# One-core channel attention with two gated layers: output products in teams from the fourth double block of layer one on, and periods in new orders

## The chip, the core and the metric

The kernel runs on one core of one Trainium2 chip, as one launch. The metric is the device time in microseconds. Five engines take part: TensorE (PE, with its weight loads PEld), VectorE (DVE), ScalarE (ACT), GpSimd (POOL) and SyncE (SP, which only issues DMAs). Each works through its own list in order, and semaphores tie the lists together.

## What is computed

```python
qn = q / (norm(q, axis=1) + 1e-6);  kn = k / (norm(k, axis=1) + 1e-6)
a = softmax(kn.transpose(0, 2, 1) @ qn / tau)        # 256 x 256, over 6016 tokens
x = v @ a                                            # 6016 x 256
xn = x / sqrt(mean(x * x) + 1e-6) * rms_g
y = (silu(xn @ w_gate) * (xn @ w_val)) @ w_out       # layer one, 256 -> 1536 -> 256
out = (sigmoid(y @ w_gate2) * (y @ w_val2)) @ w_out2 # layer two, the same sizes
```

All of it is fp32. A product is made of three matmuls (function `mm3`): each operand is split into a high part, rounded to fp32r, and a low part, the rest, and high by high, high by low and low by high are summed in one PSUM bank.

## The kernel before

**Tiling.** The tokens are cut into six double blocks of 2 x 512 columns (the third, of index 2, has 2 x 448), the hidden width of 1536 into twelve slices f of 128. One **period** handles one slice of one double block.

**Gate and value products by seven for eight.** For a double block, gate and value of a slice need eight products; `period` makes them with seven. PE runs them in the order 11, S1, (the fourth product of the period before), T2, 12, T3, S4; bank Z takes 11, T2, T3 one upon the other, bank B takes S1 and S4. Between them Z is read out: ACT copies it into A (L747, after 11), into g1 (L772, after T2) and into D (L792, after T3); then DVE adds Z and e5, the copy of B, into v1 (L798), and B into g1 (L804). ACT turns g1 into a gate (L733), and DVE multiplies gates and values (L551, L553). The next period's 11 goes into the bank Z that v1 has read, its S1 into the bank that the addition into g1 has read: PSUM has two banks `g` for Z and B, two `v`, two `y` and two `at`.

**Output products.** Double blocks 0 and 1 of layer one run plainly, block by block. Double blocks 2 to 5 of layer one run in periods whose output products are plain: four a period (`out_mm`), of two split values (L750, L775), 33 matmuls a period with the seven. In layer two the output products are made in **teams**: a team is six slices (half a double block), and its 3 x 7 products stand for 3 x 8. They follow in the six periods of the next half, 3 in an odd period and 4 in an even one, 31.5 matmuls a period on average. Each needs a source of its own: ACT casts it to its high part (L618, `split_high`), DVE subtracts to get the low part (L626, `split_low`). Sums of sources are made by DVE (`first_sum`, L559) or by DMAs that accumulate, issued by POOL (`more`, L571). `gather` adds the products into the result tiles r, and `send` (L652) stores them. The double blocks of layer two run in the order 0, 1, 3, 4, 5, 2.

**What surrounds it.** The weights of layer two come from DRAM for every slice (`gw_load`, L500, two DMAs of 448 KB, into three buffer pairs), those of the teams' output products by `ow_load` (L584). The operands of the next double block are loaded in its predecessor's first period (`pair_load`), three sums of them are made on POOL after the third (`pair_sums`, L398), a fourth later, and they are split one by one (`pair_high` L366, `pair_low` L369). During layer one, six loads `out_load` bring in the output weights of layer two, ACT and DVE split them, POOL sums them, and they are stored in `od`. The order of all this is the order of the statements in `period`; `slots` hang further work on named points of it.

Of the kernel before, what the change touches and what calls it, by code (L numbers as in the profile page):

```python
# [25 lines left out]
def kernel(  # L26
# [71 lines left out]
    gd = [dram.tile([P, 2, NG, P], F32, name=f"gd{f}") for f in range(NF)]  # L98
    rd = [dram.tile([P, 4, P], F32, name=f"rd{i}") for i in range(NF // 2)]
    od = [dram.tile([P, 8, 2, NJ, P], F32, name=f"od{g}") for g in range(2)]  # L100
# [24 lines left out]
    def conversion(l, f):  # L125
# [45 lines left out]
        def sums():  # L171
            t = w["t"]
            if l:
                nc.sync.dma_start(out=rd[f // 2][:, f % 2 * 2 : f % 2 * 2 + 2], in_=t[:, OUT:])
# [42 lines left out]
        def stored():  # L217
            if l:
                nc.sync.dma_start(out=gd[f][:, 0], in_=f32(w["h"]))
                nc.sync.dma_start(out=gd[f][:, 1], in_=f32(w["l"]))  # L220
# [217 lines left out]
    def hidden(name):  # L438
        return ip3.tile([P, 512], F32R, tag=name, name=name)
# [49 lines left out]
    stream0 = [(0, p, f) for p in range(PLAIN, NP) for f in range(NF)]  # L489
    stream1 = [(1, p, f) for p in (0, 1, 3, 4, 5, 2) for f in range(NF)]  # L490
    stream = stream0 + stream1
    HALF = NF // 2
    teams = [(p, g) for _, p, f in stream1[::NF] for g in range(2)]
    gw = {}

    def gw_load(n):
        if n < len(stream1):
            gw[stream1[n]] = [wp.tile([P, NG, P], F32R, tag=f"w{e}{n % 3}", name="gw") for e in "hl"]
            for e, t in enumerate(gw[stream1[n]]):
                nc.sync.dma_start(out=f32(t), in_=gd[stream1[n][2]][:, e])  # L500

    def product(ps, it, i, a, start, stop=True):
# [4 lines left out]
        ch, cl = gw[it] if l else (wh[0, f], wl[0, f])  # L507
# [4 lines left out]
    def out_load(i):  # L512
        odd["t"] = sp.tile([P, 4, P], F32, tag="t1", name="ot")
        nc.sync.dma_start(out=odd["t"], in_=rd[i])

    def out_store(i, h, lo, first):
        g, j = divmod(i, NJ)
        for e, t in enumerate((h, lo)):
            nc.sync.dma_start(out=od[g][:, first : first + 4, e, j], in_=f32(t))

    def out_split(i):
        odd["h"] = sp.tile([P, 4, P], F32R, tag="t2", name="oh")
        nc.scalar.copy(odd["h"], odd["t"])

    def out_low(i):
        lo = sp.tile([P, 4, P], F32R, tag="ol", name="ol")
        nc.vector.tensor_sub(lo, odd["t"], f32(odd["h"]))
        out_store(i, odd["h"], lo, 0)

    def out_sums(i):  # L530
        w11, w21, w12, w22 = (odd["t"][:, u] for u in range(4))
# [4 lines left out]

    def sums_low(i):
        lo = sp.tile([P, 4, P], F32R, tag="ol", name="ol")
        nc.vector.tensor_sub(lo, odd["t"], f32(odd["h"]))
        out_store(i, odd["h"], lo, 4)  # L540
# [14 lines left out]
    def first_sum(n):  # L555

        w = hw[stream1[n][1]]
# [3 lines left out]
    def third_sum(n):  # L561

        w = hw[stream1[n][1]]
# [15 lines left out]
    def ow_load():  # L579
        i, k = divmod(ow_n[0], len(KINDS))  # L580
        if i < len(teams):
            tag = ("wh3", "wl3", "wh4", "wl4")[ow_n[0] % 4]
            t = wp.tile([P, 2, NJ, P], F32R, tag=tag, name="ow")
            nc.sync.dma_start(out=f32(t), in_=od[teams[i][1]][:, PLACE.index(KINDS[k])])  # L584
# [7 lines left out]
    def team_start(i):  # L592

        p, g = teams[i]
        w = hw[p]
        if g == 0:
# [8 lines left out]
            p=p, g=g, w=w, split=0, done=0, parts={},  # L605
# [5 lines left out]
    def split_high(ahead):  # L611
        while job and job["split"] < min(LAST, job["done"] + ahead):
            i = job["split"]
            k, j = divmod(i, NJ)
            a, b, c, d = job["h"][j]
            src = xs[job["x"] + j][:, : job["w"]] if KINDS[k] == "S1" else {"12": c, "S4": d, "S3": b}.get(KINDS[k], a)
            h, lo = (hidden(t)[:, : job["w"]] for t in ("hh", "hl"))
            nc.scalar.copy(h, src)  # L618
            job["parts"][i] = h, lo
            job["split"] += 1  # L620
            lows.append((i, h, lo, src))

    def split_low():
        while lows:
# [25 lines left out]
    def send(v, c, e, t):  # L650
        p, w = v["p"], v["w"]
        nc.sync.dma_start(out=out_t[c * P : (c + 1) * P, p0[p] + e * w : p0[p] + (e + 1) * w], in_=t)  # L652
# [37 lines left out]
    def period(it, pv, n, outs=()):  # L690


        s = {}
        slot = slots.popleft() if slots else {}
        outs = deque(partial(out_mm, *o, c) for o in outs for c in range(KC))
        n1 = n - len(stream0)
# [5 lines left out]
        def fourth(s):  # L702
            l, p, f = s["it"]
            w = hw[p]
            product(s["v0"], s["it"], T4, A22, False)
            gated(s["h"][:, 0, :w] if l else s["v0"], s["v0"], s["sg0"], l and f % 2)

        def split(ahead):
            if n1 >= 0:
                split_high(ahead)  # L710
                split_low()

        def out(count):
            for _ in range(count):
                if outs:
                    outs.popleft()()
                elif n1 >= 0:
                    out_product()

        if it:  # L720
            l, p, f = it
            w = hw[p]
            s["it"] = it
            act = (AF.Silu, AF.Sigmoid)[l]
            Z = gv_bank("g")[:, :w]
            product(Z, it, B11, A11, True)
            A = gv_bank("v")[:, :w]
            B = gv_bank("g")[:, :w]
            product(B, it, T1, S1, True)
        if pv:  # L730
            pl, pp, pf = pv["it"]
            pw = hw[pp]
            nc.scalar.activation(out=pv["g1"], in_=pv["g1"], func=(AF.Silu, AF.Sigmoid)[pl])  # L733
            gated(pv["v1"], pv["v1"], pv["g1"], pl and pf % 2 == 0)
        flush()
        if n1 > 0 and n1 % HALF == 0:
            team_start(n1 // HALF - 1)
        if n1 > 0 and pf % 2:
            third_sum(n1 - 1)
        split(2)  # L740
        if not it:
            while job["done"] < LAST:
                split(3)
                out_product()
                flush()
            return
        nc.scalar.copy(A, Z)  # L747
        if pv and pl == 0:
            hh1, hl1 = hidden("hh"), hidden("hl")
            nc.scalar.copy(hh1[:, :pw], pv["v1"])  # L750
            nc.vector.tensor_sub(hl1[:, :pw], pv["v1"], f32(hh1[:, :pw]))  # L751
            hid[pl, pp, 1, pf] = hh1, hl1
            fourth(pv)
        e5 = sp.tile([P, 512], F32, tag="e5", name="e5")[:, :w]
        if pv and pl:
            nc.scalar.copy(e5, B)
            if n1 > 0:
                split_high(3)
            fourth(pv)
            gw_load(n1 + 2)  # L760
            split_low()
            if pf % 2 == 0:
                first_sum(n1 - 1)
        at("early")
        if not (pv and pl):
            nc.scalar.copy(e5, B)
        else:
            out(1 if n1 % 2 == 0 else 0)
# [4 lines left out]
        if pv and pl == 0:  # L773
            hh0, hl0 = hidden("hh"), hidden("hl")
            nc.scalar.copy(hh0[:, :pw], pv["v0"])  # L775
            nc.vector.tensor_sub(hl0[:, :pw], pv["v0"], f32(hh0[:, :pw]))
            hid[pl, pp, 0, pf] = hh0, hl0
        flush()
        if n1 % 2 == 0:
            split(3)  # L780
        if n1 >= 0:
            out(2 if outs else 1)
            at("DVE")
        s["sg0"] = ip2.tile([P, 512], F32, tag="sg", name="sg")[:, :w]
        nc.scalar.activation(out=s["sg0"], in_=A, func=act)  # L785
        if n1 < 0:
            out(2)
            at("ACT")
            at("DVE")
# [3 lines left out]
        if l:  # L793
            s["h"] = h_tile()
            s["v1"] = s["h"][:, 1, :w]
        else:
            s["v1"] = sp.tile([P, 512], F32, tag="t0", name="v1")[:, :w]
        nc.vector.tensor_add(s["v1"], Z, e5)  # L798
        flush()
        if n1 >= 0:  # L800
            split_high(3)
            at("ACT")
        product(B, it, B22, S4, False)
        nc.vector.tensor_add(s["g1"], s["g1"], B)  # L804
        split_low()
        if n == len(stream) - 1:
            out(2)
            fourth(s)
        else:
            out(max(2, len(outs)))  # L810
        at("end")
        return s

    with tc.manual_schedule():
# [255 lines left out]

        pv = None
        outs = [(0, b // 2, b % 2, f) for b, f in items[-SKEW:]]
        for n, it in enumerate([*stream, None]):
            if it and it[2] == 0:
                slots.clear()
                slots.extend({} for _ in range(NF))
                if n <= len(stream0):
# [12 lines left out]
            if 6 <= n < 6 + 6 * NF // 2 and n % NF % 6 == 0:  # L1090
                i = n // 6 - 1
                slots[0].setdefault("end", []).append(partial(out_load, i))
                slots[1].setdefault("ACT", []).append(partial(out_split, i))
# [55 lines left out]
```

## Time and profile before

| | us |
|---|---|
| median of three runs (lowest, highest) | 1226.77 (1225.41, 1227.59) |
| the profiled execution's own time | 1227.86 |
| its span, first to last instruction | 1225.8 |
| PE busy in the span | 1178.7 (96%) |
| DVE, ACT, POOL busy | 911.7, 847.5, 281.1 |

The span is cut below at ACT's copy L772 of the first period of each double block, so that one stretch holds twelve periods. "x397" is a count of instructions that touch the stretch, one more than belong to it.

### The profile page before, as it was taken

How to read it: one execution, taken by the hardware profiler on the slowest of the kernel's cores; microseconds unless marked ns; L12 is line 12 of the kernel's file. 1: busy time of each engine (PE TensorE's matmuls, PEld its weight loads, DVE VectorE, ACT ScalarE, POOL GpSimd, SP SyncE). 2: the span in 40 equal slices, each digit the busy share in tenths (PEclk: the TensorE clock that was granted, in tenths of full speed). 3: DMA queues.
4: the chain of work that ended last, by engine and by line, in shares of the span. 5: the costliest groups of instructions: out<-in, count | busy, mean ns of one | idle time of the engine just before them, and what ended most of it. 6: DMA issues, size and time to landing. Idle time of an engine off the chain costs nothing.

```text
span 1225.8 us, 15986 instructions
## 1 busy us (share of the span) xinstructions
PE 1178.7 (96%) x5290; PEld 966.1 (79%) x5290; DVE 911.7 (74%) x1382; ACT 847.5 (69%) x1591; POOL 281.1 (23%) x327
## 2 busy tenths in 40 slices
PE   8898999999999999999999999999999999999997
PEld 7787777788899788888888677777777777778895
DVE  6798888876566566666665577887887888887877
ACT  6665667765566676677666677677777777777775
POOL 0043655553200200200200111311311311311121
PEclk9899999999999999999999999999999999999999
DMA  9662434766301301201430578988988988988995
GB/s 334 245 221 87 131 107 158 260 224 207 111 1 28 97 26 35 95 26 35 155 99 1 168 200 248 263 247 244 267 251 239 275 246 239 277 239 248 271 251 140
DMA packets 100946, 214.43 MB, mean 175 GB/s; under 512 B 10240, under 2 KB 35840, under 8 KB 100864
## 3 DMA queue, kind: packets, MB, share of 16 engines
q1 hardware_dynamic: 86896, 188.65, 46.2%
q0 software_dynamic: 13824, 24.65, 11.1%
q8 instruction: 41, 0.67, 0.2%
q14 instruction: 41, 0.34, 0.1%
q10 hardware_dynamic: 144, 0.13, 0.0%
HBM read 150.87 MB, written 37.88 MB: 154 GB/s over the span
## 4 chain that ended last, share of the span: by engine, by line
PE 62%; DVE 11%; ACT 4%; issue 4%; DMA 1%; POOL 0%; SPq 0%; DVEq 0%; ACTq 0%; POOLq 0%
PE g L107 10%; PE g L108 9%; PE g L109 9%; PE v L107 4%; PE v L108 4%; PE y L108 4%; PE v L109 4%; PE y L109 4%; PE y L107 4%; PE at L108 3%; PE at L109 3%; PE at L107 3%; DVE hl L626 2%; DVE g L804 2%; ACT v L792 1%
## 5 line engine op out<-in xcount | busy, mean ns | idle before, releaser
L571 POOL DMA_DIRECT2D hs<-hs x96 | 83.6, 914 | 466.1 <-DVE hl L626 197.3
L626 DVE TENSOR_TENSOR hl<-hs,hh 128x512 fp32r<-128x512 f32 (+1 forms) x216 | 152.5, 714 | 20.5 <-ACT hh L618 19.7
L733 ACT ACTIVATE g<-g 128x512 f32<-128x512 f32 (+1 forms) x120 | 74.7, 623 | 121.9 <-DVE g L804 121.9
L618 ACT CAST hh<-hs 128x512 fp32r<-128x512 f32 (+1 forms) x216 | 130.1, 609 | 4.6 <-PE y L109 1.4
L792 ACT COPY v<-g 128x512 f32<-128x512 f32 (+1 forms) x120 | 67.2, 560 | 65.8 <-PE g L109 65.1
L772 ACT COPY g<-g 128x512 f32<-128x512 f32 (+1 forms) x120 | 69.4, 578 | 44.7 <-PE g L109 44.0
L798 DVE TENSOR_TENSOR hs<-g,e 128x512 f32<-128x512 f32 (+1 forms) x72 | 48.9, 680 | 50.1 <-ACT v L792 50.1
L804 DVE TENSOR_TENSOR g<-g,g 128x512 f32<-128x512 f32 (+1 forms) x120 | 79.7, 664 | 0.0
L107 PE MATMUL g<-xh,gw 128*128 128x512 f32 x180 | 73.0, 405 | 5.7 <-DVE hs L798 4.9
L785 ACT ACTIVATE sg<-v 128x512 f32<-128x512 f32 (+1 forms) x120 | 71.1, 592 | 3.7
L107 PE MATMUL g<-qh,wh 128*128 128x512 f32 x168 | 66.8, 397 | 6.6 <-ACT wh L187 5.3
L798 DVE TENSOR_TENSOR v<-g,e 128x512 f32<-128x512 f32 (+1 forms) x48 | 32.4, 675 | 53.9 <-ACT v L792 53.9
L747 ACT COPY v<-g 128x512 f32<-128x512 f32 (+1 forms) x120 | 68.0, 567 | 4.8 <-PE g L109 0.3
L108 PE MATMUL g<-xl,gw 128*128 128x512 f32 x180 | 70.3, 391 | 0.0
L109 PE MATMUL g<-xh,gw 128*128 128x512 f32 x180 | 70.2, 390 | 0.0
L109 PE MATMUL g<-qh,wl 128*128 128x512 f32 x168 | 66.3, 395 | 1.9 <-DVE wl L196 1.9
L108 PE MATMUL g<-ql,wh 128*128 128x512 f32 x168 | 66.0, 393 | 0.0
L108 PE MATMUL y<-hl,ow 128*128 128x512 f32 (+1 forms) x144 | 57.2, 397 | 9.1 <-DVE hl L626 9.0
L451 ACT CAST hh<-v 128x512 fp32r<-128x512 f32 x48 | 28.1, 585 | 48.5 <-DVE v L449 48.5
L107 PE MATMUL v<-qh,wh 128*128 128x512 f32 x144 | 57.9, 402 | 3.3 <-DVE hl L457 3.3
L751 DVE TENSOR_TENSOR hl<-v,hh 128x512 fp32r<-128x512 f32 (+1 forms) x48 | 32.7, 681 | 32.4 <-ACT hh L750 32.4
L109 PE MATMUL v<-qh,wl 128*128 128x512 f32 x144 | 56.6, 393 | 0.0
(230 smaller groups left out, 3650.2 us busy)
## 6 DMA issues: line engine op xcount, KB each, us to landing
gw<-gd SPq DMA_DIRECT2D x144, 448.0 KB, 5.5
ow<-od SPq DMA_DIRECT2D x84, 384.0 KB, 5.1
hs<-hs POOLq DMA_DIRECT2D x80, 256.0 KB, 6.7
wraw<-in_w_dram SPq DMA_DIRECT2D x24, 768.0 KB, 5.4
vraw<-in_v_t_dram SPq DMA_DIRECT2D x11, 512.0 KB, 3.8
gd<-w2h SPq DMA_DIRECT2D x12, 448.0 KB, 2.6
gd<-w2l SPq DMA_DIRECT2D x12, 448.0 KB, 3.5
yd<-yo SPq DMA_DIRECT2D x20, 256.0 KB, 2.9
```

What stands on the lines that cost most here:

```text
L107: nc.tensor.matmul(ps, sh, mh, start=start, stop=False, skip_group_check=more)
L108: nc.tensor.matmul(ps, sh, ml, start=False, stop=False, skip_group_check=more)
L109: nc.tensor.matmul(ps, sl, mh, start=False, stop=stop, skip_group_check=more)
L571: nc.gpsimd.dma_start(out=to, in_=t, accum_op=ALU.add)
L618: nc.scalar.copy(h, src)
L626: nc.vector.tensor_sub(lo, src, f32(h))
L733: nc.scalar.activation(out=pv["g1"], in_=pv["g1"], func=(AF.Silu, AF.Sigmoid)[pl])
L772: nc.scalar.copy(s["g1"], Z)
L785: nc.scalar.activation(out=s["sg0"], in_=A, func=act)
L792: nc.scalar.copy(D, Z)
L798: nc.vector.tensor_add(s["v1"], Z, e5)
L804: nc.vector.tensor_add(s["g1"], s["g1"], B)
```

## The change

The teams now begin at double block 3 of layer one: three double blocks more. Of the ten that run in periods, double block 2 of layer one alone keeps `period` and the plain output products; the other nine go through `team_period`, which reads the order of its steps from a table: EVEN and ODD by the period's number, NONE in the first six periods, where there is no team yet. So:

- The three double blocks need 54 matmuls fewer: PE's list has 5137 in place of 5191. For each of their six teams they need the casts, low parts, sums and gathers that teams need. In all, ACT gets 72 instructions more, DVE 114, POOL 72 (48 of them accumulating DMAs), SP 180 DMAs.
- Layer one's weights for the slices are stored to DRAM during double block 2 (`store_w`) and loaded per slice like layer two's; its output weights are summed and split there too, six loads more.
- Sources are split up to four products ahead, with four buffers each for high and low parts, where it was two or three products and three buffers. A call of `split_high` or `split_low` handles one source, and the table has seven or so calls a period.
- In the first six periods every odd one uses the banks `at` for Z and B.
- The loads of layer two's output weights are moved: one at the end of slice 9 and one at the end of slice 11, split one period later.

```diff
-    stream0 = [(0, p, f) for p in range(PLAIN, NP) for f in range(NF)]
-    stream1 = [(1, p, f) for p in (0, 1, 3, 4, 5, 2) for f in range(NF)]
+    alone = [(0, PLAIN, f) for f in range(NF)]
+    joint = [(0, p, f) for p in range(PLAIN + 1, NP) for f in range(NF)]
+    joint += [(1, p, f) for p in (0, 1, 3, 4, 5, 2) for f in range(NF)]
...
-        return ip3.tile([P, 512], F32R, tag=name, name=name)
+        return ip3.tile([P, 512], F32R, tag=name, name=name, bufs=4)
...
-    def split_high(ahead):
-        while job and job["split"] < min(LAST, job["done"] + ahead):
-            i = job["split"]
+    def split_high():
+        if not job or job["split"] >= min(LAST, job["done"] + 4):
+            return
+        i = job["split"]
...
+    EVEN = (
+        "part1 gate 11 h1 gw S1 cpA lo hi third hi P4 flush lo"
+        " e5 early first T2 12 h0 cpG hi lo sg lo flush hi out"
+        " DVE lo T3 part0 cpD ACT hi S4 v1 end g1 hi lo out"
+        " out hi lo out"
+    ).split()
...
+        def bank(j):
+            return (at_bank, j) if n < HALF and n % 2 else (gv_bank, "g")
...
+        for step in (EVEN, ODD)[n % 2] if n >= HALF else NONE:
+            do.get(step, partial(at, step))()
...
+            if 0 < n // NF < 4 and f == NF - 3:
+                u = 2 * (n // NF - 1)
+                slots[0].setdefault("end", []).append(partial(out_load, 1, u))
+                out_weights(1, u, slots[1], slots[2])
+                slots[2]["end"].append(partial(out_load, 1, u + 1))
+            if 1 < n // NF < 5 and f == 0:
+                out_weights(1, 2 * (n // NF - 1) - 1, slots[0], slots[1])
```

In the table's words, hi and lo are one call of `split_high` and `split_low`, P4 is the fourth product of the period before, cpA, cpG, cpD are ACT's three copies of Z, h0 and h1 the two gated values of the period before, out is one output product, end, early, ACT and DVE are the points for the slots.

**First place: ACT in two periods without output products.** Before, in layer two's first double block (v is A or D, e5 the copy of B, g1 and sg the two gates):

```order
L747 COPY v_6618<-g_6614 128x512
L756 COPY e5_6626<-g_6619 128x512
L772 COPY g1_6644<-g_6614 128x512
L785 ACTIVATE sg_6646<-v_6618 128x512
L792 COPY v_6651<-g_6614 128x512
L366 CAST qh_6499<-xs_6608 128x512
L733 ACTIVATE g1_6644<-g1_6644 128x512
L747 COPY v_6664<-g_6660 128x512
```

Now, in double block 3 of layer one:

```order
L807 COPY v_4374<-at_4366 128x512
L841 ACTIVATE g1_4345<-g1_4345 128x512
L807 COPY e5_4384<-at_4370 128x512
L807 COPY g1_4396<-at_4366 128x512
L365 CAST xh_4248<-xs_4357 128x512
L816 ACTIVATE sg_4399<-v_4374 128x512
L807 COPY v_4404<-at_4366 128x512
L807 COPY v_4420<-g_4412 128x512
```

Z and B of this period lie in `at`, those of the next in `g` again, and the gate stands behind the copy into A instead of ahead of it.

**Second place: POOL about the three sums of the next double block's operands** (the accumulating DMAs are of `hs`, the sums `xs`), in double block 1 of layer two. Before:

```order
L571 DMA hs_6824<-hs_6896 128x512
L571 DMA hs_6977<-hs_7048 128x512
L571 DMA hs_7126<-hs_7196 128x512
L398 TENSOR_TENSOR xs_7460<-xl_7304,xl_7294 128x512
L398 TENSOR_TENSOR xs_7462<-xl_7306,xs_7460 128x512
```

Now:

```order
L566 DMA hs_7478<-hs_7557 128x512
L566 DMA hs_7927<-hs_8023 128x512
L566 DMA hs_7629<-hs_7710 128x512
L397 TENSOR_TENSOR xs_8094<-xl_7940,xl_7930 128x512
L397 TENSOR_TENSOR xs_8096<-xl_7942,xs_8094 128x512
L397 TENSOR_TENSOR xs_8098<-xl_7942,xl_7940 128x512
L566 DMA hs_7778<-hs_7849 128x512
```

Before, the sums stood behind the accumulation of the last of the three sources of kind S2 (hs_7126); now they stand behind that of the second (hs_7629) and ahead of that of the third.

**Third place: DVE beside these sums.** Now, from the low part that the accumulation into hs_7629 waits for (hl are low parts, hs_8023<-v_8018 is h0, hs_8092<-g_8040 is v1, g1_8074 the addition into g1, the last row is h1):

```order
L622 TENSOR_TENSOR hl_8056<-hs_7629,hh_8055 128x512
L546 SCALAR_TENSOR_TENSOR hs_8023<-v_8018,sg_8009 128x512
L812 TENSOR_TENSOR hs_8092<-g_8040,e5_8065 128x512
L845 TENSOR_TENSOR g1_8074<-g1_8074,g_8049 128x512
L622 TENSOR_TENSOR hl_8087<-hs_7778,hh_8086 128x512
L622 TENSOR_TENSOR hl_8112<-hs_7557,hh_8111 128x512
L546 SCALAR_TENSOR_TENSOR hs_8092<-hs_8092,g1_8074 128x512
```

Three instructions that read PSUM follow the low part, and only then two further low parts. What stood there before is shown with its times in the rows below (rows 5): a low part, h0, a low part, a sum of two sources, v1.

## Rows read from the trace of the kernel before

**Rows 1.** The page: busy time, share of the span and instructions of each engine.

```profile
PE 1178.7 (96%) x5290; PEld 966.1 (79%) x5290; DVE 911.7 (74%) x1382; ACT 847.5 (69%) x1591; POOL 281.1 (23%) x327
```

**Rows 2.** Stretches: length, busy us (instructions) by engine, granted clock, DMA share, GB/s.

```profile
core 0: us, PE busy (x) PEld busy (x) DVE busy (x) ACT busy (x) POOL busy (x), PEclk, DMA share, GB/s
406.08:497.58 91.50, 90.15 (x397) 74.19 (x396) 55.78 (x86) 60.78 (x110) 10.19 (x12) 1.00 0.17 51
497.58:588.08 90.50, 90.42 (x397) 74.19 (x396) 56.21 (x86) 61.00 (x109) 10.23 (x12) 1.00 0.17 53
588.08:678.62 90.54, 90.36 (x397) 74.19 (x396) 55.01 (x84) 60.00 (x108) 7.62 (x8) 1.00 0.26 86
678.62:762.91 84.29, 79.49 (x331) 60.77 (x330) 60.08 (x93) 61.41 (x112) 15.26 (x16) 1.00 0.75 213
762.91:853.40 90.49, 87.96 (x379) 70.34 (x378) 75.68 (x116) 67.39 (x126) 19.87 (x21) 1.00 0.88 253
...
1034.38:1124.38 90.00, 87.79 (x379) 70.34 (x378) 74.79 (x116) 66.90 (x126) 19.26 (x21) 1.00 0.89 253
1124.38:1225.77 101.39, 93.48 (x429) 78.82 (x427) 77.74 (x135) 67.63 (x134) 17.96 (x21) 0.99 0.82 225
```

**Rows 3.** Timeline: start, length, engine, line, operation, [idle before it]; PE, eighteen matmuls apart.

```profile
775.64 0.39 PE L107 MATMUL y<-hh,ow 128*128 128x512 f32 x1
...
779.72 0.39 PE L107 MATMUL y<-hh,ow 128*128 128x512 f32 x1
```

**Rows 4.** Timeline of a period without output products, in layer two's first double block.

```profile
692.60 0.59 ACT L772 COPY g<-g 128x512 f32<-128x512 f32 x1 [0.78 <-PE g L109]
692.86 0.39 PE L109 MATMUL v<-xh,gw 128*128 128x512 f32 x1
693.24 0.50 PE L107 MATMUL g<-xh,gw 128*128 128x512 f32 x1
693.59 0.40 PE L108 MATMUL g<-xl,gw 128*128 128x512 f32 x1
693.83 0.40 PE L109 MATMUL g<-xh,gw 128*128 128x512 f32 x1
694.26 0.57 ACT L792 COPY v<-g 128x512 f32<-128x512 f32 x1 [0.38 <-PE g L109]
694.86 0.69 DVE L798 TENSOR_TENSOR hs<-g,e 128x512 f32<-128x512 f32 x1 [2.24 <-ACT v L792]
695.60 0.50 PE L107 MATMUL g<-xh,gw 128*128 128x512 f32 x1 [0.69 <-DVE hs L798]
```

**Rows 5.** Timeline beside POOL's three sums, DVE and POOL with the PE rows that wait.

```profile
783.03 2.33 DVE L626 TENSOR_TENSOR hl<-hs,hh 128x512 fp32r<-128x512 f32 x1
783.18 1.62 POOL L398 TENSOR_TENSOR xs<-xl 128x512 f32<-128x512 f32 x1
...
784.88 1.64 POOL L398 TENSOR_TENSOR xs<-xl,xs 128x512 f32<-128x512 f32 x1
...
785.28 0.68 DVE L553 TENSOR_TENSOR hs<-v,sg 128x512 f32<-128x512 f32 x1
...
785.89 1.18 DVE L626 TENSOR_TENSOR hl<-hs,hh 128x512 fp32r<-128x512 f32 x1
...
787.00 1.78 DVE L559 TENSOR_TENSOR t<-hs 128x512 f32<-128x512 f32 x1
...
788.70 0.68 DVE L798 TENSOR_TENSOR hs<-g,e 128x512 f32<-128x512 f32 x1
789.30 0.68 DVE L666 TENSOR_TENSOR r<-y,r 128x512 f32<-128x512 f32 x1
789.43 0.50 PE L107 MATMUL g<-qh,gw 128*128 128x512 f32 x1 [0.95 <-DVE hs L798]
```

**Rows 6.** Waits from 762.91 to 853.40 us: who for whom, us, times, longest; PE's weight loads.

```profile
PEld y L108 <- DVE hl L626: 2.1, 2, 1.3
...
PEld g L107 <- DVE hs L798: 1.4, 1, 1.4
PEld g L107 <- ACT v L747: 1.4, 3, 0.5
...
PEld g L107 <- DVE g L804: 0.9, 2, 0.7
```

**Rows 7.** A load of output weights and ACT's wait for it, in double block 3 of layer one.

```profile
411.45 0.37 SPq L514 DMA_DIRECT2D ot<-rd  x1
...
417.44 0.62 ACT L523 CAST oh<-ot 128x512 fp32r<-128x512 f32 x1 [2.32 <-DMA ot<-rd]
```

**Rows 8.** The page's DMA issues: count, KB each, median us from issue to landing.

```profile
gw<-gd SPq DMA_DIRECT2D x144, 448.0 KB, 5.5
ow<-od SPq DMA_DIRECT2D x84, 384.0 KB, 5.1
hs<-hs POOLq DMA_DIRECT2D x80, 256.0 KB, 6.7
```

**Rows 9.** Landing times of line L571's accumulating DMAs from 762.91 to 1124 us.

```profile
DMA to landing us min/median/max: 4.8/6.7/8.9
```

More of the change, by code (lines that the diff above doesn't have):

```diff
@@ L700, in at @@
                 fn()
[L702 to L718, printed above, removed]
@@ L754, in period @@
-        e5 = sp.tile([P, 512], F32, tag="e5", name="e5")[:, :w]
[L755 to L768, printed above, removed]
+        l, p, f = it
+        w = hw[p]
@@ L772, in period @@
         nc.scalar.copy(s["g1"], Z)
[L773 to L783, printed above, removed]
-        s["sg0"] = ip2.tile([P, 512], F32, tag="sg", name="sg")[:, :w]
[L785 to L789, printed above, removed]
+        if pv:
+            parts(pv, 0, pv["v0"])
+        s["sg0"] = ip2.tile([P, 512], F32, tag="sg", name="sg")[:, :w]
+        nc.scalar.activation(out=s["sg0"], in_=A, func=AF.Silu)
+        for _ in range(2):
+            outs.popleft()()
+        at("ACT")
+        at("DVE")
         product(Z, it, T3, S3, False)
@@ L792, in period @@
         nc.scalar.copy(D, Z)
-        if l:
+        s["v1"] = sp.tile([P, 512], F32, tag="t0", name="v1")[:, :w]
+        nc.vector.tensor_add(s["v1"], Z, e5)
+        product(B, it, B22, S4, False)
+        nc.vector.tensor_add(s["g1"], s["g1"], B)
+        while outs:
+            outs.popleft()()
+        at("end")
+        return s
+    EVEN = (
[4 rows of a table added]
+    ).split()
+    ODD = (
[4 rows of a table added]
+    ).split()
+    NONE = (
+        "11 S1 cpA gate h1 P4 third part1 T2 e5 12 flush h0 first"
+        " gw early part0 out out cpG ACT out sg T3 cpD out S4 end"
+        " DVE g1 v1"
+    ).split()
@@ new lines, in team_period, with new, at, out @@
+    def team_period(it, pv, n, outs):
+        l, p, f = it
+        w = hw[p]
+        pl, pp, pf = pv["it"]
+        joined = "h" in pv
+        acts = (AF.Silu, AF.Sigmoid)
+        s = {"it": it}
+        slot = slots.popleft() if slots else {}
+        outs = deque(partial(out_mm, *o, c) for o in outs for c in range(KC))
+        if n and n % HALF == 0:
+            flush()
+            team_start(n // HALF - 1)
+        def new(name, make, *args):
+            s[name] = make(*args)[:, :w]
+            return s[name]
+        def at(point):
+            for fn in slot.get(point, ()):
+                fn()
+        def out():
+            if outs:
+                outs.popleft()()
+                outs.popleft()()
+            else:
+                out_product()
+        def copied(name, make, args, src):
+            nc.scalar.copy(new(name, make, *args), s[src])
+        def valued():
@@ new lines, in team_period, with team_end @@
+        for step in (EVEN, ODD)[n % 2] if n >= HALF else NONE:
+            do.get(step, partial(at, step))()
+        return s
+    def team_end(pv, n):
+        fourth_product(pv)
+        fourth_gated(pv)
+        nc.scalar.activation(out=pv["g1"], in_=pv["g1"], func=AF.Sigmoid)
+        gated(pv["v1"], pv["v1"], pv["g1"], False)
+        third_sum(n - 1)
+        flush()
+        team_start(n // HALF - 1)
+        while job["done"] < LAST:
+            for _ in range(4):
+                split_high()
+                split_low()
+            out_product()
+            flush()
@@ L1069, with out_weights, store_w @@
                     pair_low(*first, i)
+        def out_weights(l, i, one, two):
+            for slot, first in ((one, 0), (two, 4)):
+                steps = [partial(out_high, l, i), partial(out_low, l, i, first)]
+                slot.setdefault("end", []).extend(steps if first else [*steps, partial(out_sums, l, i)])
+        def store_w(f):
+            for e, t in enumerate((wh[0, f], wl[0, f])):
+                nc.sync.dma_start(out=gd[0][f][:, e], in_=f32(t[:, :NG]))
+        out_load(0, 0)
         pv = None
@@ L1106 @@
             pv = s
-            outs = [(*it[:2], e, it[2]) for e in (1, 0)] if it and it[0] == 0 else []
+            outs = [(*it[:2], e, it[2]) for e in (1, 0)] if n < len(alone) else []
 def kernel(**inputs):
```

244 lines of the change are left out of this document (131 added, 113 removed), and 4 rows, old and new, of the table ODD.

## The prediction, made before the changed kernel was run

> **What bounds the kernel now.** I read the page's first part, then the stretches of twelve periods, then the timeline and the waits inside one stretch. PE is busy 96% of the span, DVE 74% [rows 1], so time is won where PE has fewer matmuls or waits less. The stretches price both [rows 2, 3]. Eighteen matmuls take 779.72 - 775.64 = 4.08 us, 0.2267 us each, at a granted clock of 1.00, the level of 2.4 GHz. A plain double block has 396 matmuls (x397 less the one that straddles the cut), so 89.8 us without a gap; the three of layer one that run in periods take 91.50, 90.50 and 90.54. They lose 3.3 us in all. A double block with teams has 378, so 85.7 us, and takes 90.49: it loses 4.8. The first one, whose first six periods have no output products to fill with, has 330, 74.8 us, and takes 84.29: it loses 9.5. So **teams save 4.1 us of matmuls a block today and give all of it back in waits.** That is the main thing to see: making three more blocks in the present order would bring almost nothing, and the change is worth what its new orders take out of the waits.
>
> Where the 4.8 us lie [rows 6]: PE's weight loads wait 2.1 us for low parts (two waits), 1.4 + 0.9 for v1 and for the addition into g1, which free the banks for the next period, and 1.4 (three waits) for the copy A. Those add to 5.8, a little over the loss, since a weight load can wait under a running matmul.
>
> **The change part by part.**
>
> *Matmuls.* 54 fewer, 12.2 us. The floor of everything from 406.08 on is now one first block, seven full ones and the last: 74.8 + 7 x 85.7 + 101.4 = 776.0 us, where the stretches add to 819.7. The last block (2 x 448 columns and the tail without cover) I leave at its 101.4 in the sum; it may gain up to 2. So 43.7 us are to be had, less what the new orders still lose.
>
> *First block: 2.0 us lost.* In a period without output products PE loses in two places [rows 4]. Between 12 and T3 it waits for the copy g1: 692.86 to 693.24 is 0.38 in place of 0.23, and the next step 0.35: 0.27 us a period. Between S4 and the next 11 it waits for v1: from T3's last matmul to ACT's copy 0.43, to v1 0.60, to the next 11 0.74, together 1.77 us, of which one matmul and S4 cover 0.91; with the slow restart about 1.0 a period. The odd periods' banks `at` take the second away, since the next 11 finds another bank free; the first stays. Five such periods lose 1.4, and I add 0.6 for the period in which the first team starts.
>
> *The steady period.* The same 1.77 us must now be covered by one matmul, S4 and two output products in an odd period, 0.23 + 0.68 + 1.36 = 2.27, and three in an even one, 2.95: 0.5 and 1.2 us to spare, if DVE is free for v1. The copies A and g1 have three and two products of 0.68 behind them for 1.07 us, 0.5 to spare each, and ACT has at most one cast ahead of A, where the waits for A came from two. Low parts are due four products ahead, so the 2.1 us for them should go. DVE can bear it: 115 instructions a block, one every 0.60 us (788.70, 789.30) [rows 5], are 69 of 85.7 us. What is late next is then v1 wherever DVE falls behind by over 0.5 us.
>
> *POOL's sums: 1.2 us lost a block.* While POOL makes its sums, three DVE instructions with two SBUF inputs last 2.33, 1.18 and 1.78 us in place of 0.68, 3.2 us in all, and v1 comes late: PE waits 0.95 [rows 5]. An instruction that reads PSUM (L553 at 785.28) is untouched beside a running sum. Now h0, v1 and the addition into g1, all readers of PSUM, stand where the sums begin, and only the low parts after them can meet the third sum. One such meeting costs up to 1.65 us; less the 0.5 to spare, 1.2. Seven blocks: 8.4. The ends: 0.3 a block if it is absorbed like the rest, and 3 if two or three meet as before.
>
> The Trainium skill (page "SBUF — State Buffer", section "Who interferes with whom") says that a DVE instruction with two SBUF inputs and a GpSimd instruction that reads SBUF exclude each other, the later one waiting in full, and that one with a single SBUF input is left alone. By that rule, the trace agrees: 2.33 us beside one sum, 0.68 beside another. Taken to its end it speaks against this change, and that is the last rival.
>
> *Loads of output weights: 1.5 us lost.* A load landed 6 us after its issue and held ACT for 2.3, at a DMA share of 0.17 [rows 7, 2]. ACT's queue behind it (gate, copies) is held too, and DVE behind its low part. Now the share is 0.9, but from the end of one period to the end of the next lie 6 to 7 us: 5.5 us of landing [rows 8] just fit. Six loads at 0.25 each; the ends are 0 and 5.
>
> *DMAs.* The layer-one blocks now carry layer two's traffic, at 0.88 x 90.5 / 85.7 = 0.93 of the engines. A slice's weights are asked for about 12 us before their use (8 in the first six periods), and land in 5.5; accumulating DMAs land in 8.9 at the latest [rows 9], the casts that read them stand about 11 us behind. I put this at nothing, hidden under those leads. The stores of weights and the six further loads lie in double block 2 of layer one, where the next stretches show a DMA share of 0.17 and DVE and ACT busy 61 and 66%; nothing too. The tail keeps its chain.
>
> *Sum.* 43.7 - 2.0 - 8.4 - 1.5 = 31.8 us. The profiled execution took 1227.86 (span 1225.8), 1.1 over the median; 1226.8 - 31.8 = **1195 us**.
>
> **The rivals.**
>
> *Half of it.* The orders remove the waits for low parts and for A, but v1 stays late in two or three periods a block: 3 us a block, 4 in the first, 4 for loads: 43.7 - 21 - 4 - 4 = 15 us, 1212. For it: DVE holds 115 instructions in strict order, and gathers and operand splits come in lumps. Against it: 16 us a block of free DVE.
>
> *The waits only move.* 4.8 a block and 9.5 in the first, as today: 43.7 - 33.7 - 9.5 = 0.5, so 1226. It would mean that 54 matmuls fewer are worth nothing, as three of today's plain blocks against teams show. Against it: two of today's kinds of wait have a place in the order that is gone.
>
> *Slower, by POOL against DVE.* The place is the periods in which POOL makes four sums a block of 1.6 us each. If each holds up a DVE instruction for its whole length and none of it is absorbed, a block loses 6.6 us: eight blocks 53, against 43.7 to be had, with 2 for loads 1238. It decides at 5.5 us a block. For it: teams bring low parts to three blocks more, and POOL has 72 instructions more. Against it: beside the sums today 3.2 us of stretch became 1.0 of waiting for v1.
>
> **How the numbers follow.** 1195, from 1184 (0.3 a block, no wait for loads, 2 gained in the last) to 1204: 0.65. Half of it, to 1214: 0.20. Only moved: 0.05. Slower: 0.10. The range leaves out the slower cases and a little at the low end: 1184 to 1214. A measurement can tell about 0.2%, 2.5 us, from no change; by that, faster 0.85, same 0.05, slower 0.10.
>
> **What would show it.** Twelve periods of a full block take 87 us and not 90.5, in layer one as in layer two. The periods without output products take 5.0 us and not 6.05, PE waiting there for the copy g1 alone. No waits for low parts are left; v1 is waited for once a block, beside POOL's sums, with one stretched DVE instruction. ACT waits for loads of output weights under 1 us each. The prediction is wrong if blocks take 89 us or more: then the rows to look at are v1's waits, casts waiting for accumulating DMAs, and ACT behind a load.

## The result and the profile after

| | before | after |
|---|---|---|
| median, us (lowest, highest), taken together | 1227.18 (1225.41, 1227.87) | 1195.67 (1195.11, 1196.88) |
| the profiled execution's span, us | 1225.8 | 1193.8 |

The ratio is 0.9747, 95% interval 0.9730 to 0.9764: 31.5 us less, where 31.8 were forecast. One further execution of a kernel below, `ahead5`, took 6553 us and is left out of every comparison; nothing here shows why. The total hides two errors that cancel, and the stretches show them. The page's busy line of after, against [rows 1]:

```profile
PE 1155.0 (97%) x5236; PEld 957.0 (80%) x5236; DVE 966.5 (81%) x1496; ACT 888.2 (74%) x1663; POOL 336.1 (28%) x399
```

The stretches of after, with the columns of [rows 2], cut at ACT's copy into g1 (L807) in each double block's first period: the first joint block (the first with `team_period`), the next two of layer one and layer two's first, two more of layer two's full ones, and the last.

```profile
404.70:479.81 75.11, 74.92 (x321) 59.35 (x320) 59.03 (x92) 59.20 (x112) 17.00 (x18) 1.00 0.84 247
479.81:569.83 90.02, 88.17 (x379) 71.76 (x378) 75.32 (x120) 70.53 (x131) 24.87 (x28) 0.98 0.97 284
569.83:659.69 89.86, 86.92 (x379) 70.54 (x378) 76.66 (x120) 70.64 (x130) 25.29 (x28) 1.00 0.98 283
659.69:749.95 90.26, 87.50 (x379) 70.38 (x378) 75.05 (x118) 70.95 (x130) 22.40 (x24) 1.00 0.94 272
749.95:835.98 86.03, 85.99 (x379) 70.85 (x378) 72.70 (x116) 68.71 (x126) 19.07 (x20) 1.00 0.93 266
835.98:922.01 86.03, 85.99 (x379) 70.84 (x378) 72.71 (x116) 68.71 (x126) 19.07 (x20) 1.00 0.93 266
...
1093.58:1193.80 100.22, 92.72 (x432) 81.13 (x430) 78.07 (x138) 69.38 (x136) 19.14 (x22) 0.97 0.83 231
```

Read them against the floor of 378 matmuls, 85.7 us. Layer two's full blocks behind its first lose 0.3 us where 4.8 were lost before: PE hardly stands still. The three blocks ahead of them have the same 378 matmuls and lose 4.3, 4.2 and 4.6, 13.0 us, where layer one's three plain blocks lost 3.3. So **of the 12.2 us that 54 matmuls are worth, 9.7 are lost again beyond what the plain blocks lost, and most of the gain comes from the orders in the blocks that had teams already.**

Who waits, in each of layer two's next two blocks (columns as in [rows 6]; the sole row left):

```profile
PEld g L107 <- DVE hs L812: 0.5, 1, 0.5
```

And in the first of the three slow blocks:

```profile
PEld g L107 <- ACT v L807: 2.9, 3, 2.3
PEld g L107 <- DVE hs L812: 0.2, 1, 0.2
```

The longest of these lies in the block's second period. Its timeline (start, length, engine, line, operation, idle time before it and what ended it):

```profile
483.50 1.20 SPq L528 DMA_DIRECT2D od<-o  x2
...
493.38 0.62 ACT L521 CAST o<-o 128x512 fp32r<-128x512 f32 x1 [3.17 <-DMA od<-o]
...
494.18 0.69 DVE L524 TENSOR_TENSOR o<-o 128x512 fp32r<-128x512 f32 x1 [2.25 <-DMA od<-o]
...
494.95 0.57 ACT L807 COPY v<-g 128x512 f32<-128x512 f32 x1
...
495.58 0.68 PE L107 MATMUL g<-xh,gw 128*128 128x512 f32 x1 [1.85 <-ACT v L807]
```

ACT does not wait for a load, as the prediction had it, but for a **store**. The second split of layer two's output weights writes into the tile of the first split, whose store was issued 9.9 us before. Behind the cast in ACT's queue stand the gate and the copy A, which PE needs. The next block has the same stop, 3.60 us before its cast at 583.82. All 48 stores of the splits in one view, with who waited for them (us, times) and from issue to landing; three of ACT's four waits, 9.5 us, lie in the three slow blocks:

```profile
  ACT o L521: 10.2, 4
  DVE o L524: 7.0, 4
busy tenths in 40 slices 0000000000000000000000000000000000000000
DMA to landing us min/median/max: 2.2/4.6/10.3
```

### The profile page after: what moved, and what is told of

Read it like the earlier page. It is cut to its first block, busy times and chain, and to the rows that moved or that the text cites. A ratio compares the mean times of both kernels' runs of the same rounds, so it can differ in the third digit from the quotient of the medians.

```text
span 1193.8 us, 16672 instructions
## 1 busy us (share of the span) xinstructions
PE 1155.0 (97%) x5236; PEld 957.0 (80%) x5236; DVE 966.5 (81%) x1496; ACT 888.2 (74%) x1663; POOL 336.1 (28%) x399
## 4 chain that ended last, share of the span: by engine, by line
PE 68%; DVE 4%; DMA 4%; issue 3%; ACT 3%; POOL 0%; DVEq 0%; SPq 0%; ACTq 0%; POOLq 0%
PE g L107 11%; PE g L108 10%; PE g L109 10%; PE v L107 5%; PE v L108 5%; PE v L109 5%; PE y L108 4%; PE y L107 4%; PE y L109 4%; PE at L107 4%; PE at L108 4%; PE at L109 4%; DMA od<-o 2%; DVE hl L622 1%; DMA hs<-hs 1%
## 5 line engine op out<-in xcount | busy, mean ns | idle before, releaser
L566 POOL DMA_DIRECT2D hs<-hs x144 | 125.6, 924 | 573.5 <-DVE hl L622 417.2
L622 DVE TENSOR_TENSOR hl<-hs,hh 128x512 fp32r<-128x512 f32 (+1 forms) x324 | 223.2, 700 | 25.4 <-ACT hh L614 24.5
L614 ACT CAST hh<-hs 128x512 fp32r<-128x512 f32 (+1 forms) x324 | 195.2, 613 | 23.7 <-PE at L109 6.5
L807 ACT COPY v<-g 128x512 f32<-128x512 f32 (+1 forms) x210 | 119.0, 567 | 63.7 <-PE g L109 60.4
L107 PE MATMUL g<-xh,gw 128*128 128x512 f32 x240 | 94.8, 395 | 4.6 <-ACT v L807 3.3
L109 PE MATMUL g<-xh,gw 128*128 128x512 f32 x240 | 93.7, 390 | 0.0
L108 PE MATMUL y<-hl,ow 128*128 128x512 f32 (+1 forms) x216 | 84.5, 391 | 1.8 <-DVE hl L622 1.8
L107 PE MATMUL y<-hh,ow 128*128 128x512 f32 (+1 forms) x216 | 84.4, 391 | 1.9 <-ACT hh L614 1.9
L109 PE MATMUL y<-hh,ow 128*128 128x512 f32 (+1 forms) x216 | 83.8, 388 | 0.0
L807 ACT COPY g<-g 128x512 f32<-128x512 f32 (+1 forms) x105 | 61.2, 583 | 26.5 <-PE g L109 26.2
L845 DVE TENSOR_TENSOR g<-g,g 128x512 f32<-128x512 f32 (+1 forms) x105 | 70.3, 669 | 5.7 <-PE g L109 5.7
L107 PE MATMUL g<-qh,gw 128*128 128x512 f32 (+1 forms) x171 | 66.8, 390 | 3.0 <-ACT v L807 2.3
L108 PE MATMUL g<-ql,gw 128*128 128x512 f32 (+1 forms) x171 | 65.8, 385 | 0.0
L109 PE MATMUL g<-qh,gw 128*128 128x512 f32 (+1 forms) x171 | 65.8, 385 | 0.0
L107 PE MATMUL at<-hh,ow 128*128 128x512 f32 (+1 forms) x162 | 63.1, 389 | 0.0
L108 PE MATMUL at<-hl,ow 128*128 128x512 f32 (+1 forms) x162 | 63.0, 389 | 0.0
L109 PE MATMUL at<-hh,ow 128*128 128x512 f32 (+1 forms) x162 | 62.9, 388 | 0.0
```

The costliest lines, as they stand in the source:

```text
L107: nc.tensor.matmul(ps, sh, mh, start=start, stop=False, skip_group_check=more)
L108: nc.tensor.matmul(ps, sh, ml, start=False, stop=False, skip_group_check=more)
L109: nc.tensor.matmul(ps, sl, mh, start=False, stop=stop, skip_group_check=more)
L566: nc.gpsimd.dma_start(out=to, in_=t, accum_op=ALU.add)
L622: nc.vector.tensor_sub(lo, src, f32(h))
L807: nc.scalar.copy(new(name, make, *args), s[src])
```

## The experiments

What is compared between kernels is the ratio to the kernel before on the same chip (it took 1224.7, 1224.1 and 1228.2 us beside the three groups of runs), or a stretch from the first joint period on: what lies ahead of it took 404.7 to 411 us in the profiles, for kernels that are alike there.

**What brings the gain: the extension, the look-ahead or the orders.** First the extension in the old orders.

```diff
-        for step in (EVEN, ODD)[n % 2] if n >= HALF else NONE:
+        for step in OLD:   # the steps of the kernel before, look-ahead two and three
-            return (at_bank, j) if n < HALF and n % 2 else (gv_bank, "g")
+            return gv_bank, "g"
```

> The three added team blocks with their loads and stores as in the changed kernel, but every joint period in the order of the kernel before (look-ahead of two and three, banks g throughout). Theory (in the old order the waits eat the matmuls): 1226 us, within 2 of the kernel before; the first joint block takes 84 us, the other seven full ones 90 to 91 in either layer. Rival (the matmuls count whatever the order): 12.2 us off, 1215. Were the stores of output weights to stop ACT here as they do in the changed kernel, some 7 us would come on top of either.

Measured: 1237.88 us, ratio 1.0105 (1.0079 to 1.0131): 1% over the kernel before. The waits eat the matmuls, as the theory said (a block of layer two takes 90.4 us), and the stop for the store comes on top, longer than in after (at 502.40 ACT's cast had waited 4.88 us). A block of layer two, then the second and third joint blocks:

```profile
773.78:864.22 90.44, 87.94 (x379) 70.33 (x378) 75.68 (x116) 67.35 (x126) 19.86 (x21) 1.00 0.89 253
...
487.53:584.23 96.70, 90.75 (x379) 72.25 (x378) 78.63 (x120) 69.55 (x130) 24.84 (x29) 0.96 0.93 264
584.23:677.82 93.59, 88.24 (x379) 70.25 (x378) 78.55 (x120) 69.43 (x130) 24.88 (x29) 1.00 0.95 272
```

Then the new orders without the extension.

```diff
-    alone = [(0, PLAIN, f) for f in range(NF)]
-    joint = [(0, p, f) for p in range(PLAIN + 1, NP) for f in range(NF)]
-    joint += [(1, p, f) for p in (0, 1, 3, 4, 5, 2) for f in range(NF)]
+    alone = [(0, p, f) for p in range(PLAIN, NP) for f in range(NF)]
+    joint = [(1, p, f) for p in (0, 1, 3, 4, 5, 2) for f in range(NF)]
```

> The new orders alone: teams from the first block of layer two on, as before the change, all of layer one's double blocks plain. Theory: the orders bring nearly all, since the three added team blocks of the changed kernel take 90.0 us each where plain blocks took 90.8: 272.5 - 270.1 = 2.4 us more than the changed kernel, 1198, with 75 us for the first joint block and 86 for the full ones. Rival (the extension is worth its 54 matmuls once the orders are right): 12.2 us more, 1208.

Measured: 1198.23, ratio 0.9775 (0.9753 to 0.9798). The changed kernel has 0.9747 in the first comparison and 0.9781 in `again`, below. A full block of layer two loses as little as in after:

```profile
752.55:838.56 86.01, 85.98 (x379) 70.84 (x378) 72.73 (x116) 68.65 (x126) 19.03 (x20) 1.00 0.93 266
```

The orders alone bring nearly all of the gain, and in the totals the extension as it stands can't be told from nothing; its 54 matmuls are not worth the 10 us that separate the rival's 1208 from the 1198 measured. The stretches give it about 2 us: the four blocks from layer one's fourth double block to layer two's first take 349.4 us here and 345.3 in after, and of the difference 2.3 are ten matmuls that the new order makes ahead of the cut.

Third, the old orders with the new look-ahead, teams in layer two only.

```diff
-            "hi2": lambda: highs(2),
-            "hi3": lambda: highs(3) if n else None,
+            "hi2": lambda: highs(4),
+            "hi3": lambda: highs(4) if n else None,
```

> Teams in layer two alone, every joint period in the order of the kernel before, but parts made up to four products ahead in place of two and three. The prediction's account (2.1 of the 4.8 us a block are low parts, due four products ahead): five full blocks, 10 us less than the kernel before, 1214, with v1 and the copy A still late. If the look-ahead alone is the gain: 1198, as the new orders. If a longer look-ahead in the old places only puts more casts ahead of the copies: 1225 or more.

Measured: 1234.12, ratio 1.0055 (1.0035 to 1.0076): 0.5% over the kernel before, the third case. The waits of one block (855.96 to 947.05, 91.09 us):

```profile
PEld g L107 <- ACT v L807: 4.2, 8, 1.0
PEld y L108 <- DVE hl L620: 2.1, 2, 1.3
```

In the old places a longer look-ahead leaves the 2.1 us for low parts as they were and raises the waits for the copy A from 1.4 [rows 6] to 4.2: more casts stand ahead of it in ACT's queue, up to four in a row (from 897.53) where the kernel before had one or two.

Fourth, the new orders with the look-ahead of the old.

```diff
-        if not job or job["split"] >= min(LAST, job["done"] + 4):
+        if not job or job["split"] >= min(LAST, job["done"] + 3):
```

> The changed kernel with parts made at most three products ahead and not four. The prediction gives the 2.1 us a block of waits for low parts to the look-ahead: 7 full blocks, 15 us more, 1210. Rival (the places of the parts in the new orders are what counts): 1196 to 1198.

Measured: 1233.32, ratio 1.0071 (1.0050 to 1.0092). Both expectations were far off. A layer-two block takes 90.37 us, and its waits are all for low parts:

```profile
PEld y L108 <- DVE hl L622: 3.8, 4, 1.7
PEld at L108 <- DVE hl L622: 1.4, 2, 0.7
```

By the table, with a limit of three a `hi` would find the limit reached more often, and the part would be made a call later, nearer to its product; that is a reading of the table, and no run counts the calls. **The look-ahead and the orders are worth nothing apart (1.0055 and 1.0071) and 2.2 to 2.5% together.** Two things are not separated by this: `look3` keeps the extension and the banks `at`, `old4` has neither, and both have the four buffers, whose number no run changes.

**The changed kernel again**, the yardstick of three runs on another chip.

> The changed kernel itself, as a yardstick on the chip of the next three runs: 1195.7, or 0.975 of the kernel before, if chips agree; the stretches from 405 us on within 1 us of those of its first profile.

Measured: 1197.61, ratio 0.9781 (0.9759 to 0.9803). From the first joint period on it takes 1196.4 - 408.49 = 787.9 us, against 1193.8 - 404.70 = 789.1.

**The first joint block.**

```diff
-            return (at_bank, j) if n < HALF and n % 2 else (gv_bank, "g")
+            return gv_bank, "g"
```

> The changed kernel without the odd periods' banks `at` in the first joint block (banks g throughout, the order of the steps kept). The prediction's first-block term says that these banks take away a wait for v1 of about 1.0 us in each of five periods without output products: 5 us more, 1200.7, periods of 6.1 us in place of 5.1. Rival (the new order of the steps is enough): 1196, periods of 5.1.

Measured: 1202.31, 4.7 us over `again`. A period without output products takes 6.20 us (418.72 to 424.92), and 5.10 in after:

```profile
418.72:424.92 6.20, 5.35 (x22) 3.79 (x21) 2.54 (x5) 3.35 (x6) 4.90 (x4) 1.00 0.68 192
```

So the banks `at` are worth about what I gave them, five periods of 1.0 us. The wait that they take away is put down to the addition into g1 (7.7 us in six waits for DVE g L845 in that block), which DVE now does just ahead of v1, and not to v1 as the prediction had it.

**POOL's sums.**

```diff
-        t = ip3.tile([P, 512], F32, tag="yo", name="xs")[:, :w]
-        nc.gpsimd.tensor_sub(t, *ab)
-        sums[out] = t
+        sums[out] = ab[0]
```

> The changed kernel with POOL's sums of operand quarters left out (one quarter stands in for each sum, so that part of the result is not computed). The prediction's term of 1.2 us for each of seven blocks: 8.4 us less, 1187. What the trace after shows (0.33 us in each layer-two block, about 1.0 in the period after the sums in three blocks of layer one): 5 us less, 1191. If DVE's stretch costs PE nothing: 1196.

Measured: 1191.40, 6.2 us under `again`; from the first joint period on 1188.8 - 404.18 = 784.6 us against 787.9, so 3.3 of it lie in the joint periods; the rest lies ahead of them, where like kernels differ by as much. Layer two's blocks take 85.70, the floor, with no wait left: the sums' price there is 0.33 us a block, a quarter of the 1.2 forecast.

```profile
745.64:831.34 85.70, 85.70 (x379) 70.94 (x378) 71.94 (x116) 68.62 (x126) 13.87 (x16) 1.00 0.93 267
```

Then the same sums a third of a period later, in the kernel `ahead` below.

```diff
-                    slots[2].setdefault("end", []).append(partial(pair_sums, *nxt))
+                    slots[3].setdefault("early", []).append(partial(pair_sums, *nxt))
```

> As ahead5, and POOL's sums of operand quarters begin one third of a period later. If they then lie beside instructions that read PSUM, the losses after the sums go (0.33 us in three blocks of layer two, 0.65 to 1.1 in three of layer one): 4 us under ahead5, 1187. If they meet other low parts: the same or up to 4 us over it.

Measured: 1207.64, ratio 0.9844 (0.9820 to 0.9868), 15 us over `ahead5`, where at most 4 were expected. This is the mechanism of the prediction's slower rival, at another place: the sums now meet a gated value with two SBUF inputs and low parts, and PE waits for the v1 behind them.

```profile
867.69 2.52 DVE L546 SCALAR_TENSOR_TENSOR hs<-hs,g 128x512 f32<-128x512 f32 x1
...
868.03 1.62 POOL L397 TENSOR_TENSOR xs<-zl,ql 128x512 f32<-128x512 f32 x1
...
869.73 1.63 POOL L397 TENSOR_TENSOR xs<-zl,xs 128x512 f32<-128x512 f32 x1
870.13 0.67 DVE L680 TENSOR_TENSOR r<-r,y 128x512 f32<-128x512 f32 x1
870.73 1.18 DVE L622 TENSOR_TENSOR hl<-hs,hh 128x512 fp32r<-128x512 f32 x1
...
876.07 0.50 PE L107 MATMUL g<-xh,gw 128*128 128x512 f32 x1 [1.91 <-DVE hs L812]
```

The period about them takes 9.04 us in place of 7.13 (870.12 to 879.16 here, 857.72 to 864.85 in after). L680, which reads PSUM, keeps its 0.67 beside a running sum. The Trainium skill (page "SBUF — State Buffer", section "Who interferes with whom") names just this pair, a DVE instruction with two SBUF inputs against a GpSimd instruction that reads SBUF. By that rule, the trace agrees: 2.52 us beside the sum, 0.68 for the like instruction at 856.27 in after.

**The stop for the store.** Place in the queue, or the buffer? First the place: the first split, and so its store, goes ahead of the four operand loads on SP, which were issued between 480.04 and 482.48 in after.

```diff
-                    slots[0].setdefault("end", []).append(partial(pair_load, *nxt, own))
+                    if 1 < n // NF < 5:
+                        out_weights(1, 2 * (n // NF - 1) - 1, slots[0], slots[1])
+                    slots[0].setdefault("end", []).append(partial(pair_load, *nxt, own))
```

> The changed kernel with one queue position altered: in the first period of a double block the first split of layer two's output weights, and so its store, stands ahead of the four loads of the next operands on SP. If ACT's wait of about 3 us in the next period comes from the store being queued behind those loads, it goes in three blocks, 2.5 us each: 1188. If the store is slow because the DMA engines are full (share 0.97 in these blocks) and not because of its place, the wait stays: 1195 to 1196.

Measured: 1193.21, ratio 0.9727 (0.9697 to 0.9757), where 1188 was expected. From the first joint period on it takes 1191.5 - 409.87 = 781.6 us, 7.5 less than after, as expected; the total shows less of it, since the part ahead took 409.87 us here and 404.70 in after. Once more, over more executions:

> The kernel with the store of the first split ahead of the operand loads once more, with more rounds: 0.972 to 0.974 of the kernel before, 1191, against 0.975 to 0.978 for the changed kernel; from the first joint period on 781 to 782 us.

Measured: 1192.61, ratio 0.9705 (0.9678 to 0.9732), **the lowest ratio of this study.** The interval still touches that of after (0.9730 to 0.9764), so the stretches are the better witness: from the first joint period on it takes 1191.4 - 410.95 = 780.4 us, 8.7 less than after and 7.5 less than `again`. Its three blocks, and the waits that end at ACT's second cast in all of them (us, times):

```profile
485.94:572.85 86.91, 86.67 (x379) 70.58 (x378) 76.25 (x120) 70.66 (x130) 25.29 (x28) 1.00 0.99 293
572.85:659.56 86.71, 86.71 (x379) 70.52 (x378) 75.77 (x120) 70.83 (x130) 25.30 (x28) 1.00 0.99 294
659.56:748.12 88.56, 87.18 (x379) 70.46 (x378) 75.06 (x118) 71.18 (x130) 22.44 (x24) 1.00 0.95 277
...
  DMA od<-o: 2.5, 3
```

The store is issued no earlier: it goes out at 489.64, 78.7 us from the cut where the first joint period begins, and 78.8 in after. The loads now follow it, from 491.22 on, and it lands in time. The DMA engines are as full as before (0.99), so with the traffic unchanged it was the place of one store in the queue. What is left of the loss in the first two blocks, 1.2 and 1.0 us, are short waits of 0.7 us at most, for v1 and the copy A above all. The third block keeps 1.28 us in which ACT loads a table for the second layer's gate (660.82 in after).

The traffic has its part too. In `orders` the second splits rewrite a stored tile in the same way, with the loads ahead of the store in the same order (496.08 to 498.09) and with only 5.4 us from the store's issue to the time when ACT was ready for the next cast, but most of them lie in plain blocks at a DMA share of 0.13 to 0.32. There ACT waits 1.0 us in all, and the stores land sooner:

```profile
DMA to landing us min/median/max: 2.3/2.4/6.0
```

So it takes three things to make the stop: the tile, the place and full DMA engines. The first two are shown by an edit each; for the third this comparison alone speaks, and `orders` differs in more than its traffic.

Then the buffer: the second split gets a tile of its own and writes its low part over the loaded tile. To make room for it, three filler tiles that the kernel never reads (2.2 KB a partition) go.

```diff
-    const.tile([P, 224], F32, name="fill")
-    wp.tile([P, 80], F32, name="fill")
-                ops["fill"] = sp.tile([P, 248], F32, name="fill")
...
+            a, b, c, d = (ip3.tile([P, 512], F32, tag="yo", name="o", bufs=4) for _ in range(4))
+            odd["t"], odd["h"], odd["l"], odd["h2"], odd["l2"] = (c, b, a, d, c) if i % 2 else (a, b, c, d, a)
```

> The changed kernel with a buffer of its own for the second split's high part, its low part written over the loaded tile (unused filler tiles of 2.2 KB are given up for it). Theory (ACT waits for the store because the second split writes into the stored buffer): the three waits go whatever the store takes, 2.5 us a block: 1188, blocks that end in layer one at 87.5 us in place of 90. Rival (the wait only shows a late ACT; DVE and the DMA engines are the limit in these blocks): 1194 to 1196, blocks still at 89 or more.

Measured: 1203.34, ratio 0.9814 (0.9790 to 0.9837): slower than after and far from the 1188 expected, though ACT's waits for the stores fell to 1.4 us, none of them in the three blocks. So the fillers alone were taken away:

> The changed kernel without its three unused filler tiles (2.2 KB a partition), nothing else changed; operands then lie at other addresses. The kernel with buffers of its own for the second split (it gave the fillers up) took matmuls of 0.231 to 0.234 us in joint periods in place of 0.2267. Theory (the addresses do that): 13 us more than the changed kernel, 1210. Rival (it came with the extra buffer or the rewritten tile): 1196.

Measured: 1208.65, ratio 0.9842 (0.9822 to 0.9862), as the theory had it. Two blocks of `nofill`, one with each set of operand tiles:

```profile
843.70:931.72 88.02, 88.02 (x379) 70.99 (x378) 72.78 (x116) 69.11 (x126) 19.10 (x20) 1.00 0.91 260
756.71:843.70 86.99, 86.99 (x379) 70.88 (x378) 72.91 (x116) 68.94 (x126) 19.12 (x20) 1.00 0.92 263
```

PE is busy throughout at a granted clock of 1.00, the level of 2.4 GHz, and waits for nobody, but a block takes 2.0 or 1.0 us more than the 86.03 of after. That is what hid the gain in `own`. Against `nofill` that gain shows in the second and third joint blocks, first of `own`, then of `nofill`:

```profile
483.70:573.04 89.34, 88.56 (x379) 70.63 (x378) 77.04 (x120) 71.13 (x130) 25.02 (x28) 1.00 0.97 286
573.04:660.41 87.37, 87.37 (x379) 70.58 (x378) 76.77 (x120) 70.83 (x131) 25.27 (x28) 1.00 0.99 292
...
484.08:575.06 90.98, 88.68 (x379) 70.64 (x378) 76.69 (x120) 71.02 (x130) 25.29 (x28) 1.00 0.96 281
575.06:666.10 91.04, 87.80 (x379) 70.56 (x378) 76.80 (x120) 70.90 (x131) 25.31 (x28) 1.00 0.97 280
```

So the two cures work on the same stop, and the shared tile is what turns a late store into a stop.

## Why the prediction was right, step by step

- **What bounds the kernel: right.** The view that blocks with teams give their saving back in waits was borne out twice: `teams` shows it for more blocks, `orders` that nearly all of the gain lies in taking the waits out.
- **Matmuls: right.** 54 fewer, x5290 to x5236, and the cadence stays.
- **First block: right in kind, 2.0 us forecast.** Periods without output products take 5.06 to 5.10 us, forecast 5.0; PE waits there for ACT's copies, 2.1 us in five waits for g1. `gonly` prices the banks at 4.7 us. The stretch has 320 matmuls and not the 330 that I counted, since the new order makes ten of them ahead of the cut: against its own 72.5 us it lost 2.6, not the 0.3 that 75.1 against 74.8 suggests.
- **The steady period: right, for half a reason.** In layer two's full blocks low parts and copies are no longer waited for. I gave the low parts to the look-ahead; `old4` and `look3` show that neither look-ahead nor order does anything alone.
- **POOL's sums: mis-sized, 8.4 us forecast.** The mechanism stands (one stretched pair a block, v1 waited for once, as forecast: 2.26 us for two low parts at 854.09). A block of layer two loses 0.33, not 1.2, since v1 stands ahead of the stretched pair (852.88) and the next v1 comes at 861.07. In all the sums cost 3.3 us by `nosums`.
- **Loads and DMAs: mis-sized the other way, 1.5 us forecast.** This is the step that failed: 1.5 us for the output weights, and of the traffic "I put this at nothing, hidden under those leads." The loads do fit: from 404 us to the last block neither ACT nor DVE nor PE waits for one, nor for an accumulating DMA, though these land in up to 11.3 us and not 8.9. (Ahead of that one load held ACT for 2.0 us, at 393.00.) But a store also has a lead to keep where its tile is rewritten, and that I had not looked for: od landed in up to 10.3 us, and from its issue at 483.50 to the time when ACT was ready for the next cast lay 6.7. `ahead5` took out 8.0 us of the 13.0 that the three blocks lose. By the sign that I set myself, blocks of 89 us or more, these three (90.0, 89.9, 90.3) count against the prediction; of the rows that I named for that case, it was ACT standing still, behind a store and not a load.
- **Last block: in its bounds**, 100.22 against 101.4, with three matmuls more in its stretch.
- **The sum.** From the first joint period on I had 776.0 + 2.0 + 8.4 + 1.5 = 787.9 us; after took 789.1. The three blocks before layer two's full ones took 270.1, with 1.2 each for the sums and 1.5 for loads I had 262.2: 7.9 too little. The four full blocks behind them took 343.6, I had 4 x 86.9 = 347.6: 4.0 too much. The first and the last took 175.3, I had 76.8 + 101.4 = 178.2: 2.9 too much. A good total, then, from terms of which two were wrong by more than half; that they cancel to 1.2 us is luck. Of the 2.9 the first block's 1.7 come from the cut alone: the ten matmuls ahead of it are worth 2.3.

## What to carry to other kernels

When a saving is put into blocks that already wait, price the waits first and alone: here the orders were worth 26 us without the extension and the extension minus 13 without the orders. Count a lead for every store whose tile is written again, as for every load, and put such a store ahead of loads that nobody needs soon. Look-ahead and order are one setting: here either alone came out 0.5 to 0.7% over the kernel before.

## What the runs showed of the hardware that I had not expected

**Tiles that nothing reads change the matmuls' pace.** Without 2.2 KB of tiles that nothing reads, 378 matmuls take 86.99 to 88.02 us in place of 85.7, all with PE busy. The edit changes nothing else, so I put it down to the addresses at which the operands then lie; the addresses themselves were not read. The Trainium skill (page "SBUF — State Buffer", section "Who interferes with whom") says that PE waits on no one; no wait is in the rows here either, but the pace differs by 1.5 to 2.7%. What in an address would do it wasn't tried. It is not behind the other differences told here: the third matmul of a product, which has nothing to wait for, lasts 389 to 390 ns on average in a block of layer two of before, after, `teams`, `orders`, `old4` and `look3`, and 395 in `nofill`.

**The same stop may or may not cost clock.** After PE's stop of 1.85 us the granted clock fell to 0.50, the level of 1.2 GHz, and came back; one microsecond to a row:

```profile
495.50:496.50 1.00, 0.92 (x3) 0.73 (x4) 1.00 (x2) 1.00 (x3) 0.72 (x2) 0.62 1.04 422
496.50:497.50 1.00, 1.00 (x4) 0.81 (x3) 1.00 (x3) 0.41 (x2) 1.00 (x2) 0.50 1.01 398
497.50:498.50 1.00, 1.00 (x4) 0.81 (x3) 0.38 (x1) 0.31 (x2) 0.98 (x3) 0.50 1.11 339
498.50:499.50 1.00, 1.00 (x4) 0.76 (x4) 0.00 (x0) 0.53 (x1) 1.00 (x1) 0.67 1.16 408
499.50:500.50 1.00, 1.00 (x6) 0.80 (x6) 0.00 (x0) 0.23 (x1) 0.92 (x2) 1.00 1.06 370
```

The next period took 8.51 us (497.15 to 505.66) where the like one a block later, 587.03 to 594.53, took 7.50. There PE had stood still for 2.25 us, longer, and the granted clock stayed at 1.00. What decides between the two stays open.
